# A long convolution with a top-2 FFN on one core: the last chunk cut into channel halves, under a new instruction order

## The chip, the cores and the metric

One core of a Trainium2 chip. The time is device microseconds of one execution, given as the median of several runs; a profile adds the trace of one execution, whose span is some 2 us shorter than the time. Executions of one kernel spread by several per cent (144.09 to 150.12 us for the changed kernel in one call), so I quote stage lengths from traces beside medians. The record calls an execution slow when it is over 1.5% above the fastest of its kernel in the same call; medians here are over all executions of a call, unless I say fast. Engines: PE multiplies matrices, DVE and ACT work on vectors, POOL is a third and slower one (an addition of 128x512 elements takes 1156 ns there and 426 on DVE, in the first profile), SP sends DMAs.

## The reference, cut to what matters

```python
h  = x + q_ln * (irfft(rfft(kv) * rfft(filter)) + kv * D)      # q_ln = layernorm(x), kv = short_conv(k) * v
r  = layernorm(h) @ w_r;  idx = top-2 tokens by r              # 2048 tokens, 640 channels
y  = (silu(sel @ w_gate) * (sel @ w_up)) @ w_down              # for the two selected tokens only
out = h + layernorm(h);   out[idx] += y * sigmoid(r[idx])
```

The rows to be selected are known only after every channel of `h` is done: the end of the convolution is on the path to everything that follows.

## The kernel before

The 640 channels go in five chunks of 128. A chunk has two forward transform stages (`S1`, `S2`), two elementwise products with the filter's spectrum (`P1`, `P2`), two inverse stages (`I1`, `I2`), a multiplication by q with an addition to x (`I2m`, `I2a`), a transposition of the new h (`T`), and Gram sums of the transposed h (`G`), which give the second layernorm's statistics and the scores. Matmul results are copied out of PSUM by ACT or DVE. Four PSUM regions are shared out by the plan.

The program is recorded as steps, and a list, `PLAN`, gives their order, the engine and the PSUM region of each; semaphores follow from the order. Each engine runs its steps in that order.

```python
# products of chunk c: two blocks of 64 frequencies, all channels
def p1(b):
    blk = slice(64 * b, 64 * b + 64)
    op("dve", lambda e: e.tensor_tensor(dst[:, :, blk], A[:, :, blk], dst[:, :, blk], ALU.mult), ...)
def p2(b): ...                         # the same for K (the swapped spectrum)
for b in range(2): p1(b)
for b in range(2): p2(b)
...
# first inverse, block gb of 32 channels: needs all frequencies, so both P1 and both P2
for gl in range(8):
    matmul(R32(bt)[...], lhsT=dst[:, g, :], rhs=G[:, 0, :], start=True, stop=False)
    matmul(R32(bt)[...], lhsT=K[:, g, :],   rhs=G[:, 1, :], start=False, stop=True)
# second inverse, tokens n0..n1, all 128 channels: needs all four copies of the first
for n2 in range(n0, n1):
    for cp in range(2):
        matmul(R32(bt)[...], lhsT=H[:, n2, cp, :], rhs=Bp[:, 16 * cp + n2, :], start=(cp == 0), stop=(cp == 1))
# (cut: copies, I2m, I2a, transposes, Gram sums, scheduler)
```

## Time and profile before

| | before |
|---|---|
| time, median of the first comparison | 152.75 us (152.32 to 154.05) |
| span of the first profile | 148.27 us |
| PE / DVE / ACT busy | 86 / 78 / 76 % |
| last forward stage begins | 99.18 us |
| last forward copy ends (point A) | 106.84 us |
| first inverse of the last chunk begins | 114.35 us, A + 7.51 |
| second inverse of the last chunk begins | 121.55 us, A + 14.71 |
| last Gram matmul ends | 131.78 us, A + 24.94 |
| from there to the end | 16.49 us |

I split the span at these points: "front" is the time to the start of the last forward stage, "segment" runs from there to the last Gram matmul, and "end" is the rest. The segment is 32.60 us here. The 40-slice part of the page shows PE's busy tenths, its granted clock and DMA:

```profile
PE   7397999958959599979999999999998979967962
...
PEclk9999999999999999999999999999999996985799
DMA  4999399937999979968865956853189934035980
```

Each digit is a slice of 3.7 us in tenths. PE is busy nearly everywhere, so a gain can come only from work that it does sooner, or at a better clock. The clock falls below full in the 34th slice (6), which lies inside the segment, and in the 36th to 38th (8, 5, 7), mostly behind it. The segment's own lines stand in the prediction.

### The profile page before, as it was taken

What the parts mean: (1) busy time and instruction counts of PE and PEld (TensorE: products, weight loads), DVE (VectorE), ACT (ScalarE), POOL (GpSimd) and SP (SyncE); (2) the same over time, 40 slices, a digit from 0 to 9 for tenths busy, and PEclk for the clock granted to TensorE, in tenths of its full rate; (3) what the DMA queues carried; (4) which work ended last, traced back from release to release, by engine and by line L of the source; (5) the groups of instructions that cost most, each with busy time, mean ns of one, the idle gap of its engine ahead of it and who ended that gap; (6) DMA issues with size and microseconds to landing.
All of it is one profiled execution on the core that took longest, in us unless ns stands there. A gap on an engine that the chain in (4) does not pass through costs nothing.

```text
span 148.3 us, 6818 instructions
## 1 busy us (share of the span) xinstructions
PE 127.6 (86%) x3087; PEld 113.3 (76%) x3087; DVE 115.0 (78%) x178; ACT 112.2 (76%) x133; POOL 31.8 (21%) x46
## 2 busy tenths in 40 slices
PE   7397999958959599979999999999998979967962
PEld 7256896657849499969989899898997879935950
DVE  0486779885898689699989998999899556478921
ACT  0596799399988958979898996889999902639910
POOL 2011004300170219067421506230600000000010
PEclk9999999999999999999999999999999996985799
DMA  4999399937999979968865956853189934035980
GB/s 108 335 287 372 78 334 393 226 81 219 257 162 240 240 205 222 230 179 304 178 137 121 213 111 147 180 206 123 47 265 337 317 111 124 4 93 171 427 322 6
DMA packets 20769, 30.07 MB, mean 203 GB/s; under 512 B 5311, under 2 KB 15748, under 8 KB 20228
## 3 DMA queue, kind: packets, MB, share of 16 engines
q1 hardware_dynamic: 20200, 28.03, 67.0%
q0 software_dynamic: 512, 1.60, 4.2%
q8 instruction: 24, 0.39, 1.2%
q14 instruction: 5, 0.04, 0.1%
q10 hardware_dynamic: 28, 0.00, 0.0%
HBM read 19.60 MB, written 2.62 MB: 150 GB/s over the span
## 4 chain that ended last, share of the span: by engine, by line
PE 49%; DMA 19%; DVE 13%; ACT 11%; issue 4%; SPq 1%; DVEq 0%
PE ps L622 9%; DMA big<-in_A_ssm_k_dram 7%; PE ps L666 6%; ACT A L350 6%; PE ps L597 5%; DMA big<-big 5%; DMA KfB<-A 4%; PE ps L729 4%; DMA q_sb<-c_F 4%; PE ps L711 3%; PE ps L712 3%; PE ps L1047 3%; DVE KfB L643 2%; PE ps L845 2%; DVE big L350 2%
## 5 line engine op out<-in xcount | busy, mean ns | idle before, releaser
L350 ACT ACTIVATE big<-ps 128x1024 bf16<-128x1024 f32 (+1 forms) x33 | 33.5, 1066 | 5.9 <-PE ps L622 5.7
L350 ACT ACTIVATE A<-ps 128x1024 bf16<-128x1024 f32 x33 | 31.5, 1036 | 3.1 <-PE ps L666 3.0
L666 PE MATMUL ps<-big,F 128*128 128x64 bf16 x640 | 22.0, 192 | 4.4 <-DVE big L350 2.2
L622 PE MATMUL ps<-F,big 128*64 128x128 bf16 x640 | 23.5, 228 | 2.5 <-DVE big L350 1.6
L666 PEld LDWEIGHTS ps<-big,F 128*128 128x128 bf16 x640 | 20.2, 97 | 5.7 <-ACT A L350 2.6
L622 PEld LDWEIGHTS ps<-F,big 128*64 128x64 bf16 x640 | 19.8, 115 | 5.3 <-DVE big L350 2.4
L711 PE MATMUL ps<-G,A 128*128 128x128 bf16 x160 | 19.2, 219 | 0.1
L712 PE MATMUL ps<-G,KfB 128*128 128x128 bf16 x160 | 19.2, 219 | 0.0
L802 POOL TENSOR_SCALAR q_sb<-x_sb,ln 128x640 bf16<-128x640 bf16 x16 | 14.1, 879 | 23.1 <-DVE A L687 11.6
L350 ACT ACTIVATE Bp<-ps 128x1024 bf16<-128x1024 f32 x16 | 15.6, 1055 | 1.1 <-PE ps L712 1.1
L711 PEld LDWEIGHTS ps<-G,A 128*128 128x128 bf16 x160 | 15.5, 98 | 0.8 <-DVE atmp L739 0.2
L350 ACT ACTIVATE q_sb<-ps 128x2048 bf16<-128x2048 bf16 (+2 forms) x7 | 9.7, 1427 | 8.3 <-PE ps L750 8.3
L712 PEld LDWEIGHTS ps<-G,KfB 128*128 128x128 bf16 x160 | 15.7, 98 | 0.0
L739 DVE TENSOR_TENSOR atmp<-q_sb,ps 128x1024 bf16<-128x1024 bf16 (+1 forms) x11 | 12.1, 1117 | 4.0 <-PE ps L729 3.8
L350 DVE COPY big<-ps 128x2048 bf16<-128x2048 bf16 (+1 forms) x10 | 11.2, 1118 | 4.5 <-PE ps L546 1.5
L607 DVE TENSOR_TENSOR big<-ps,big 128x1024 bf16<-128x1024 f32 x10 | 12.0, 1219 | 2.5 <-PE ps L597 2.4
L743 POOL TENSOR_TENSOR x_sb<-x_sb,atmp 128x512 bf16<-128x512 bf16 x8 | 9.1, 1156 | 17.2 <-DVE atmp L739 6.3
L695 DVE TENSOR_TENSOR KfB<-A,KfB 128x2048 bf16<-128x2048 bf16 x10 | 12.3, 1248 | 0.0
L687 DVE TENSOR_TENSOR A<-A 128x2048 bf16<-128x2048 bf16 x10 | 12.1, 1217 | 0.1
L729 PE MATMUL ps<-Bp,H 128*128 128x128 bf16 x160 | 11.3, 229 | 0.5 <-ACT Bp L350 0.4
L729 PEld LDWEIGHTS ps<-Bp,H 128*128 128x128 bf16 x160 | 9.9, 103 | 1.1 <-ACT Bp L350 0.5
L350 DVE CAST big<-ps 128x1024 bf16<-128x1024 f32 x8 | 9.5, 1217 | 1.5 <-PE ps L622 1.5
(131 smaller groups left out, 194.6 us busy)
## 6 DMA issues: line engine op xcount, KB each, us to landing
KfB<-A SPq DMA_DIRECT2D x6, 512.0 KB, 4.8
big<-big SPq DMA_DIRECT2D x10, 260.0 KB, 6.3
big<-in_A_ssm_k_dram SPq DMA_DIRECT2D x5, 512.0 KB, 5.1
out_dram<-q_sb SPq DMA_DIRECT2D x4, 640.0 KB, 4.7
big<-in_B_w_up_dram SPq DMA_DIRECT2D x5, 432.0 KB, 4.9
big<-in_B_w_gate_dram SPq DMA_DIRECT2D x5, 432.0 KB, 4.5
big<-in_A_k_dram SPq DMA_DIRECT2D x4, 512.0 KB, 4.2
big<-in_A_v_dram SPq DMA_DIRECT2D x4, 512.0 KB, 5.8
```

What stands on the lines that cost most here:

```text
L350: return flex(lambda e: e.activation(o, i(), ACTF.Copy), lambda e: e.tensor_copy(o, i()), reads, writes, (t_act(n), t_d2(n) if bf else t_d ...
L607: op("dve", lambda e: e.tensor_tensor(kv[:, :, 8 * hb:8 * hb + 8, :], R32(bt).rearrange("p (n g l) -> p g n l", n=8, l=4), v_T[:, 8 * hb:8 ...
L622: return e.matmul(R32(bt)[64 * cc:64 * cc + 64, 128 * gl:128 * gl + 128], lhsT=lt, rhs=F1[:, cc, :], start=True, stop=True, tile_position= ...
L666: bt = op("pe", [lambda e, kl=kl: e.matmul(R32(bt)[:, 64 * kl:64 * kl + 64].rearrange("p (s g) -> p s g", s=2), lhsT=F2[:, 16 * r + kl, :] ...
L687: op("dve", lambda e: e.tensor_tensor(dst[:, :, blk], A[:, :, blk], dst[:, :, blk], ALU.mult), reads=[buf("A2", ksl(c), r) for r in rs], w ...
L695: return lambda e: e.tensor_tensor(K[:, g0:g1, blk], A[:, g0:g1, blk], K[:, g0:g1, blk], ALU.mult)
L711: ems.append(lambda e, g=g, gl=gl: e.matmul(R32(bt)[:, 128 * gl:128 * gl + 128], lhsT=dst[:, g, :], rhs=G[:, 0, :], start=True, stop=False))
L712: ems.append(lambda e, g=g, gl=gl: e.matmul(R32(bt)[:, 128 * gl:128 * gl + 128], lhsT=K[:, g, :], rhs=G[:, 1, :], start=False, stop=True))
L729: ems.append(lambda e, n2=n2, nl=nl, cp=cp: e.matmul(R32(bt)[:, 128 * nl:128 * nl + 128], lhsT=H[:, n2, cp, :], rhs=Bp[:, 16 * cp + n2, :] ...
L739: tr.decl({"dve": lambda e: e.tensor_tensor(at, qv, R32(bt)[:, 0:128 * nn].rearrange("p (n d) -> p n d", n=nn), ALU.mult)}, qb, ab, {"dve" ...
L743: em["pool"] = [lambda e, a=a: e.tensor_tensor(xs[:, a:a + 4, :], xs[:, a:a + 4, :], at[:, a:a + 4, :], ALU.add) for a in range(0, nn, 4)]
L802: lambda e, n2=n2: e.tensor_scalar(q_sb[:, n2, :], x_sb[:, n2, :], rd[:, n2:n2 + 1], nb[:, n2:n2 + 1], op0=ALU.mult, op1=ALU.add),
```

## The change

The intent: let the last chunk's second half of channels be multiplied while the first half is already in the inverse stages, and let the residual end in small pieces.

```diff
+LASTG = True
+            def ph(h):                                  # products by halves of the channels, all frequencies
+                g = slice(NG // 2 * h, NG // 2 * h + NG // 2)
+                op("dve", lambda e: e.tensor_tensor(dst[:, g], A[:, g], dst[:, g], ALU.mult), ..., writes=[buf("P1o", h)], ...)
+                op("dve", lambda e: e.tensor_tensor(K[:, g], A[:, g], K[:, g], ALU.mult), ..., writes=[buf("P2o", h)], ...)
+            if last(c):
+                ph(0)
+                ph(1)
+                return
...
-            bt = op("pe", ems, reads=dbufs[0] + dbufs[1] + [buf("P2", c % 2, 0), buf("P2", c % 2, 1), bG], ..., name="I1%d%d" % (c, gb))
+            bt = op("pe", ems, reads=([buf("P1o", gb // 2), buf("P2o", gb // 2)] if last(c) else ...) + [bG], ..., name="I1%d%d" % (c, gb))
...
+        def b_I2h(c, h, n0, n1):                        # second inverse, 64 channels, tokens n0..n1
+            bt = op("pe", [lambda e, n2=n2, cp=cp: e.matmul(R32(bt)[...], lhsT=H[:, n2, cp, :], rhs=Bp[:, 16 * cp + n2, w * h:w * h + w], ...)
+                           for n2 in range(n0, n1) for cp in range(2)], reads=[buf("Bp", 2 * h), buf("Bp", 2 * h + 1), bH], ...)
+            ...                                         # I2m and I2a on the same half
...
-            for p_ in parts(c):
-                b_I2(c, *p_)
+            if last(c):
+                b_I2h(c, 0, 0, NB)                      # first half: all 16 token blocks
+                for p_ in parts(c):                     # second half: 8, 4, 4 token blocks
+                    b_I2h(c, 1, *p_)
+            else: ...
# cut: PLAN, replaced as a whole (559 steps before, 562 now)
```

The new list also moves things outside the last chunk. The first Gram chunk stands ahead of the last chunk's first inverse and the second between its blocks, instead of both behind it; the second chunk's filter is loaded ahead of eight token blocks of x; and the output normalizations stand elsewhere.

## The prediction

> **What bounds the kernel now.** I read the busy times first: TensorE (PE) 86% of the 148.3 us span, ScalarE (ACT) 76%, VectorE (DVE) 78%. Such averages name no bound: the 40 slices show all three at 0.9 in the middle and DVE and ACT falling to 0.2 to 0.6 after slice 30. The chain that ended last agrees:
>
> ```profile
> PE 49%; DMA 19%; DVE 13%; ACT 11%; issue 4%; SPq 1%; DVEq 0%
> ```
>
> So what a change to the last of five channel chunks is worth must be read between the last forward stage and the end of the Gram sums (the row sums and squares for the second layernorm, L845 and L850). The time-ordered list of DVE's instructions there:
>
> ```profile
> 107.15 2.48 DVE L643 COPY KfB<-A 64x4096 bf16<-64x4096 bf16 x2
> 109.66 1.23 DVE L687 TENSOR_TENSOR A<-A 128x2048 bf16<-128x2048 bf16 x1
> 110.80 2.35 DVE L695 TENSOR_TENSOR KfB<-A,KfB 128x2048 bf16<-128x2048 bf16 x2
> 113.07 1.22 DVE L687 TENSOR_TENSOR A<-A 128x2048 bf16<-128x2048 bf16 x1
> 114.21 2.34 DVE L739 TENSOR_TENSOR atmp<-q_sb,ps 128x1024 bf16<-128x1024 bf16 x2
> 118.37 1.23 DVE L350 CAST Bp<-ps 128x1024 bf16<-128x1024 f32 x1 [1.82 <-PE ps L712]
> 119.51 1.28 DVE L741 TENSOR_TENSOR x_sb<-x_sb,atmp 128x1024 bf16<-128x1024 bf16 x2
> 123.22 1.22 DVE L739 TENSOR_TENSOR atmp<-q_sb,ps 128x1024 bf16<-128x1024 bf16 x1 [2.43 <-PE ps L729]
> ```
>
> It is serial: swap 2.5 us, four products 4.6 us (each covers half the frequencies and all channels, so no inverse matmul may start before the fourth ends at 114.29), then DVE idles while PE does all 64 first-inverse matmuls, and idles again until the second inverse. The chain shows what PE did from 118.3:
>
> ```profile
> 118.33 0.31 PE ps L845 x32
> 118.64 0.28 PE ps L850 x8
> 118.92 0.25 PE ps L845 x22
> 119.17 0.83 issue
> ...
> 121.62 1.56 PE ps L729 x16
> 123.19 1.71 PE ps L750 x16
> 124.89 0.69 PE ps L729 x8
> ```
>
> The last Bp copy ends at 119.60, but the in-order PE queue holds two whole Gram chunks in front of the second inverse, which starts two microseconds late and then runs slowly. The windows tell why:
>
> ```profile
> 120.00:122.00 2.00, 2.00 (x105) 1.86 (x105) 0.79 (x2) 0.00 (x0) 0.00 (x0) 0.97 0.10 38
> 122.00:124.00 2.00, 2.00 (x22) 2.00 (x20) 0.78 (x1) 0.00 (x0) 0.00 (x0) 0.50 0.55 154
> 124.00:126.00 2.00, 2.00 (x57) 1.95 (x55) 1.51 (x3) 1.07 (x1) 0.00 (x0) 0.68 0.20 76
> ```
>
> The third figure from the right is the granted PE clock: half. The Gram sums end at 131.83; 16.5 us of dependent small steps (top-2 search, gather, FFN, row write) follow.
>
> [...] 0.50 follows a stretch of 32- and 2-column matmuls with a 0.83 us hole, and sixteen L729 matmuls take 1.56 us there, 0.89 to 1.00 elsewhere. [...] here sixteen 64-column matmuls (L666) take 0.47 us, 29 ns each, sixteen of 128 take 0.89 us, so splitting into 64 columns costs little. [...] the products take 1217 and 1248 ns on runs of 64, so halves by channel should cost the same. [...] The 0.83 us "issue" fell while DMA was 84% busy (118.2 to 120)[...].
>
> **The change, part by part.** Let A be the end of the last copy of the last forward stage (106.8 before). I lay the new order of each engine's queue out from A with durations of this trace.
>
> Products: still 4 x 1.2 us, but the first two finish channels 0 to 63. Ready at A + swap 2.5 + sign 0.1 + 2.4 = A+5.0; before, everything at A+7.5. The new order puts one residual multiply (1.2) between the pairs, so the second half is ready at A+9.2.
>
> First inverse: PE does chunk 3's four blocks, a transpose, Gram chunk 0 and chunk 3's second inverse until A+6.5; blocks 1 and 0 of the last chunk until A+8.3; Gram chunk 1 to A+9.4; blocks 2 and 3 to A+11.25 (PSUM regions come free just in time). Both Gram chunks thus move into PE's wait for products: in the old order they cost 118.33 to 121.55.
>
> Second inverse: first half 32 x 0.03 = 1.0, A+11.3 to A+12.3 (old: starts A+14.7). DVE multiplies it to A+13.5. PE meanwhile transposes chunk 3 and does eight tokens of the second half, then four, Gram 2, four (last ends A+15.3). DVE: 0.7 + 0.68 + 0.4 + 2 x 0.4 + 2 x 0.28 = 3.1 after A+13.65: residuals complete A+16.8 (my estimates for the smallest sizes, scaled from 0.42 at 512 elements). Last transposes, Gram 3 and 4: A+18.8. Added work: 32 more matmuls (1.94 against 1.78 us) and three short DVE instructions; trivial.
>
> Before, the same stretch took 131.83 - 106.8 = 25.0. Laid out with the same ideal durations it would be about 21.3: the other 3.7 are the half clock, the hole and small hand-overs. So the structure is worth 21.3 - 18.8 = 2.5 us; up to 3.7 more depends on whether the new queue avoids the cold clock. PE is nearly gapless from A to A+17 and the Gram sums are interleaved with dense matmuls, so I count half of it: 1.8. Together -4.3 us.
>
> Front: the plan is new everywhere. Summed with this trace's durations, ACT has 96.3 us of work up to its last forward copy in both orders, DVE 94.3 and 94.7 up to the swap: neither is relieved. Immediately before A, ACT gets all eight forward copies (8 x 1.03) where DVE took one, and DVE gets two transposed copies: A about 1 us later there. But the load of chunk 1's filter moves up by eight token blocks, 1.28 MB, an estimated 3.4 us at some 380 GB/s; this ended a wait of 2.5 us on ACT (29.68), and lies on the chain as "DMA big<-in_A_ssm_k_dram". I count -1 us net, the least certain term.
>
> Tail after Gram: the first four warm-up matmuls move from before the key transposes to the very end. They held up nothing (done 133.97, transposes at 134.13), and the clock was 0.50 there in spite of them. One output normalization (0.4) now stands before the row maximum and three instead of two between it and the second maximum (0.4 beyond the 0.7 of the transposes): +0.8 on the path to the gather. ACT does eight normalizations instead of seven before its table load and the sigmoid, +0.8, but the FFN's end was set by 1.12 us of "issue" at 141.86, so part hides there. Net +0.3. Weight loads are issued earlier except one up-projection and some down-projection loads; they are needed some 9 us later and land in about 5.
>
> Sum: -4.3 - 1.0 + 0.3 = -5.0 us on the span; 152.81 - 5.0 = 147.8. Hand-laid queues lose some at every hand-over, so I say 148.2.
>
> **Rivals.** (1) The clock goes cold anyway, and an instruction hole comes too: the end of the new order is still small Gram matmuls and transposes. [...] Then only structure is left, -2.5 - 1.0 + 0.3 = -3.2: about 149.6, within a hair of 2%. (2) DVE becomes the bound of the tail: 5.0 us of products and swap, the inserted multiply and nine short operations are one queue. Against: it still waits for PE at A+12.3 and twice was idle before (1.82, 2.43). If true, second-half residuals arrive 1 to 2 us later: 149.5. (3) The new front loses: loads in another order, stacked-shift DMAs, forward copies on ACT. At +2 us instead of -1: 151, called the same. (4) Everything works, clock warm and filter wait gone: 145.
>
> **Range and chances.** The front gives about +-2 us, clock and holes +-1.8, tail +-0.8; together about +-3: 145.0 to 151.4. The 2% line is 149.75; rivals 1 and 2 land just on its fast side, only a losing front or two of them together cross it. Faster 0.70, same 0.27, slower 0.03.
>
> **What would show it.** Right: two products end, then L711/L712 start some 2.5 us after the swap while the other two run; both early Gram chunks lie before the last first-inverse block; from A to the last Gram matmul 19 to 21 us instead of 25.0; clock at 1.0 until then; ACT's 2.5 us wait for the filter gone, A at or before 106.8; from Gram's end to the span's end 16 to 17.5. Wrong: A later than 108, the half clock already in the second inverse, or the last DVE residuals waiting in DVE's own queue.

## The result, and the profile after

The changed kernel takes 147.24 us (147.09 to 149.54) against 152.75 us. The ratio is 0.962, with a 95% interval of 0.956 to 0.968. Ratios are the mean time of one kernel's fast runs over that of the other's in the same rounds, so not quite the ratio of the medians. Its first profile fell on a slow execution (span 147.65 us); I read a second one (span 144.86 us) and a third (148.32, slow again). The spread is in the front and, in the third, at the end; the segment hardly moves. (A variant below with the same order up to the last Gram matmul, the output normalizations off the path, took 29.32 us for it.)

| us | before, 2 traces | changed, 3 traces |
|---|---|---|
| front | 99.18, 102.81 | 102.30, 99.30, 101.57 |
| segment | 32.60, 33.10 | 28.57, 28.75, 28.83 |
| end | 16.49, 16.44 | 16.78, 16.81, 17.92 |
| A to the first inverse | 7.51, 7.51 | 6.44, 6.34, 6.70 |
| A to the second inverse | 14.71, 14.67 | 11.19, 11.09, 11.45 |
| A to the last Gram matmul | 24.94, 25.43 | 19.97, 20.14, 20.22 |

DVE's instructions in order of time, changed kernel, second profile (start, length, engine, line, operation, tiles, shapes; in brackets idle time before and what ended it):

```profile
108.25 2.48 DVE L644 COPY KfB<-A 64x4096 bf16<-64x4096 bf16 x2
...
110.83 1.21 DVE L707 TENSOR_TENSOR A<-A 128x2048 bf16<-128x2048 bf16 x1
111.96 1.22 DVE L708 TENSOR_TENSOR KfB<-A,KfB 128x2048 bf16<-128x2048 bf16 x1
113.56 1.22 DVE L752 TENSOR_TENSOR atmp<-q_sb,ps 128x1024 bf16<-128x1024 bf16 x1 [0.37 <-PE ps L742]
114.69 1.22 DVE L707 TENSOR_TENSOR A<-A 128x2048 bf16<-128x2048 bf16 x1
115.83 1.22 DVE L708 TENSOR_TENSOR KfB<-A,KfB 128x2048 bf16<-128x2048 bf16 x1
...
120.14 2.05 DVE L770 TENSOR_TENSOR atmp<-q_sb,ps 128x1024 bf16<-128x1024 bf16 x2 [0.63 <-PE ps L764]
122.10 1.02 DVE L772 TENSOR_TENSOR x_sb<-x_sb,atmp 128x1024 bf16<-128x1024 bf16 x2
123.04 0.74 DVE L770 TENSOR_TENSOR atmp<-q_sb,ps 128x256 bf16<-128x256 bf16 x2
123.70 0.48 DVE L772 TENSOR_TENSOR x_sb<-x_sb,atmp 128x256 bf16<-128x256 bf16 x2
```

The four products still cost 1.2 us each, but the second one ends at 113.18 (A + 5.27), and PE, busy with the chunk before until then, starts the first inverse at 114.25 while the third and fourth products are still to come. The chain of waits of the same trace shows the second inverse and the last transposes and Gram matmuls (start, length, engine, line, count):

```profile
119.17 0.93 PE ps L764 x32
120.10 0.89 PE ps L777 x16
120.99 0.83 PE ps L764 x24
121.82 0.18 PE ps L877 x8
...
125.43 0.18 PE ps L877 x8
125.60 0.23 PE ps L872 x20
125.83 1.19 issue
127.02 0.25 PE ps L872 x12
...
127.46 0.26 PE ps L872 x16
```

L764 is the second inverse by halves, L777 the transposition, L872 and L877 the Gram sums. Thirty-two 64-column matmuls take 0.93 us; transposing sixteen blocks takes 0.89 us, where the kernel before needed 1.71 at a clock of 0.50. The windows have the clock third from the right, 1.00 here:

```profile
120.00:122.00 2.00, 2.00 (x62) 1.91 (x61) 1.73 (x2) 1.22 (x2) 0.00 (x0) 1.00 0.06 17
122.00:124.00 2.00, 2.00 (x111) 1.83 (x113) 2.00 (x7) 1.07 (x2) 0.00 (x0) 1.00 0.00 0
...
126.00:128.00 2.00, 0.98 (x52) 0.82 (x51) 0.26 (x1) 0.00 (x0) 0.00 (x0) 1.00 0.79 229
128.00:130.00 2.00, 0.05 (x9) 0.00 (x0) 1.90 (x9) 0.34 (x3) 0.20 (x1) 0.80 1.05 359
```

The clock stays full until after the last Gram matmul (it halves at 129.2; in the other two traces at 131.7 and 132.0, again 0.8 to 1.6 us after that matmul). In the two traces of the kernel before it halves at 121.9 and 124.9, inside the segment, for 3.4 us. What is left is one hole of 1.19 us called "issue" among the last Gram matmuls (0.91 and 0.92 in the other traces).

### The profile page after: what moved, and what is told of

It reads as the page before. It is cut to its first block, busy times and chain, and to the rows that moved or that the text cites.

```text
span 147.7 us, 6882 instructions
## 1 busy us (share of the span) xinstructions
PE 123.0 (83%) x3119; PEld 110.0 (75%) x3119; DVE 114.5 (78%) x185; ACT 109.7 (74%) x129; POOL 30.5 (21%) x45
## 4 chain that ended last, share of the span: by engine, by line
PE 53%; DMA 17%; ACT 11%; DVE 11%; issue 5%; SPq 1%; DVEq 0%
DMA KfB<-A 8%; ACT A L351 8%; PE ps L623 8%; PE ps L667 6%; PE ps L724 5%; PE ps L725 5%; DMA big<-big 5%; DMA q_sb<-c_F 4%; PE ps L742 4%; ACT big L351 3%; PE ps L777 3%; PE ps L524 3%; DVE big L351 3%; PE ps L1079 3%; PE ps L604 3%
## 5 line engine op out<-in xcount | busy, mean ns | idle before, releaser
L351 ACT ACTIVATE big<-ps 128x1024 bf16<-128x1024 f32 (+2 forms) x39 | 39.3, 1068 | 9.1 <-PE ps L623 8.8
L351 ACT ACTIVATE A<-ps 128x1024 bf16<-128x1024 f32 x31 | 29.4, 1047 | 2.4 <-PE ps L667 2.2
L725 PE MATMUL ps<-G,KfB 128*128 128x128 bf16 x160 | 18.8, 219 | 0.0
L756 POOL TENSOR_TENSOR x_sb<-x_sb,atmp 128x512 bf16<-128x512 bf16 x6 | 6.8, 1151 | 24.8 <-DVE KfB L699 13.1
L752 DVE TENSOR_TENSOR atmp<-q_sb,ps 128x1024 bf16<-128x1024 bf16 x8 | 9.7, 1218 | 2.2 <-PE ps L742 2.1
L691 DVE TENSOR_TENSOR A<-A 128x2048 bf16<-128x2048 bf16 x8 | 9.7, 1217 | 2.1 <-DMA KfB<-A 2.1
L351 DVE CAST A<-ps 128x1024 bf16<-128x1024 f32 x9 | 10.8, 1221 | 0.4 <-PE ps L667 0.3
L598 PE MATMUL ps<-diag,big 128*128 128x64 bf16 x256 | 8.6, 194 | 1.9 <-DMA big<-big 1.9
L524 PE MATMUL ps<-q_sb,cons 128*128 128x512 bf16 x20 | 6.8, 478 | 3.6 <-DMA q_sb<-c_F 3.6
L699 DVE TENSOR_TENSOR KfB<-A,KfB 128x2048 bf16<-128x2048 bf16 x8 | 9.8, 1231 | 0.0
L598 PEld LDWEIGHTS ps<-diag,big 128*128 128x128 bf16 x256 | 7.9, 98 | 2.4 <-issue 2.0
```

The costliest lines, as they stand in the source:

```text
L351: return flex(lambda e: e.activation(o, i(), ACTF.Copy), lambda e: e.tensor_copy(o, i()), reads, writes, (t_act(n), t_d2(n) if bf else t_d ...
L524: wt = op("pe", [lambda e, i=i: e.matmul(R32(wt)[:, 512 * (i % 2):512 * (i % 2) + 512], lhsT=ident, rhs=F2c[:, 0:16].rearrange("p k c m -> ...
L598: return e.matmul(R32(bt)[:, o:o + 64], lhsT=lt, rhs=diagS[:, s, h, a, :], start=(a == 0), stop=(a == 1))
L699: return lambda e: e.tensor_tensor(K[:, g0:g1, blk], A[:, g0:g1, blk], K[:, g0:g1, blk], ALU.mult)
L725: ems.append(lambda e, g=g, gl=gl: e.matmul(R32(bt)[:, 128 * gl:128 * gl + 128], lhsT=K[:, g, :], rhs=G[:, 1, :], start=False, stop=True))
L752: tr.decl({"dve": lambda e: e.tensor_tensor(at, qv, R32(bt)[:, 0:128 * nn].rearrange("p (n d) -> p n d", n=nn), ALU.mult)}, qb, ab, {"dve" ...
```

## The experiments

Line numbers of the variants are a few lower, since their lists are printed more tightly. All outputs are right. A variant with new tasks in the old places is made by giving a new `PLAN`; I show which steps move. The kernel before was timed beside each call, and its median there went from 150.70 to 153.25 us, so small differences between calls mean nothing.

**Both kernels again.**

> The changed kernel once more, for a profile in the fast state. Theory (the gain lies in the tail, from the last forward stage to the end of the Gram sums): ratio 0.955 to 0.968 as before, from the start of the last forward stage to the end of the last Gram matmul about 28 us against 32.6 in the old profile. Rival (the gain is in the front and the first profile of the changed kernel merely hid it): in a fast-state profile the last forward stage starts well before 99 us.

Measured: 147.82 us against 153.25, a ratio of medians of 0.965; the stages are in the table above. Only one of seven of the kernel before was fast, and at 147.84 us it lay among the three fast ones of the changed kernel (146.75 to 148.09). Over all calls the medians are 152.07 us (45 executions of the kernel before) and 147.56 us (15 of the changed one). The segment was as the theory said. The last forward stage started at 99.30, not well before 99: the gain isn't hidden in the front.

> The kernel before against itself: ratio 1.00 within 0.5 per cent. Its first profile was 2.4 us quicker than its median, so I expect a new profile with a span near 150.7 us; theory: the extra 2 us sit in the front as longer waits for DMA or for instructions, and the tail segment from last forward stage to last Gram matmul stays 31 to 33 us. Rival: the tail itself varies by 2 us.

Measured: 151.05 us median, and a slow profile of 152.35 us. The front took 3.6 us more than in the first profile (102.81 against 99.18) and the segment 33.10 against 32.60. So in these two traces the spread of one and the same kernel is in the front. Two traces of one kernel thus differ there by as much as I wanted to measure, and no single pair of traces can price the front. The same file against itself came out 2.2 us under the other runs of the kernel before in that call, not within the 0.5 per cent that I expected, which shows how far a median of five can be trusted here.

**Old front, new tail.** The seam is the end of the fourth chunk's forward stage, where both lists have done nearly the same steps.

```diff
-PLAN = new[0:334] + new[334:562]
+PLAN = old[0:334] + (the steps of new that are not in it, in new's order)
```

> Old order up to the end of the fourth chunk's forward stage (334 of 562 steps of the plan), then the new order with the halves. Theory of the prediction (tail -4, front -1): 148 to 149.5, ratio about 0.972. Rival all-tail: ratio 0.962. Rival all-front: ratio 0.99 to 1.00.

Measured: 147.98 us (147.89 to 151.23), median of 153.25 beside it; ratio of the medians 0.966. Segment 29.21 us (the clock halves at 128.4, 0.7 us before its end), front 99.91, end 16.78. The new tail behind the old front is as good as the whole change within what the spread allows (147.82 us in the same call). The ratio lies between the theory and the all-tail rival and doesn't part them.

**New front, old tail.**

```diff
-PLAN = old[0:334] + old[334:559]
+PLAN = new[0:334] + (the steps of old that are not in it, in old's order)
```

> New order up to the same seam, then the old order with undivided products, inverse stages and additions. Theory of the prediction: front alone is worth 1 us, 151 to 152, ratio about 0.99. Rival all-tail: 1.00. Rival all-front: 0.962 to 0.97.

Measured: 150.16 us (147.77 to 151.53), front 98.06, segment 31.49, end 16.42. The time, a ratio of medians of 0.980, lies between the theory and the all-front rival and settles neither. The segment is the instructive number. The same tail steps took 32.60 and 33.10 us behind the old front; here they took 31.49, and the clock was full:

```profile
120.00:122.00 2.00, 1.61 (x30) 1.49 (x28) 1.44 (x2) 0.04 (x1) 0.00 (x0) 1.00 0.68 187
122.00:124.00 2.00, 2.00 (x98) 1.89 (x96) 1.52 (x3) 1.84 (x1) 0.00 (x0) 1.00 0.12 43
124.00:126.00 2.00, 1.62 (x70) 1.45 (x69) 1.11 (x2) 1.51 (x2) 0.00 (x0) 1.00 0.00 0
```

The old tail can thus run without the half clock. Together with a third such trace (31.20 us, below) this parts the gain: 32.60 to 33.10 with the half clock, 31.20 to 31.49 without, so 1.1 to 1.9 us of clock; and 31.20 to 31.49 less 28.57 to 28.83, so 2.4 to 2.9 us of structure. These two traces also lack the 0.8 us hole in the early Gram sums; holes of 0.36 to 0.39 us stand elsewhere.

I could have read the parts from PE alone. The whole segment of the kernel before, of this one and of the changed one (after the length: PE busy, PE weight loads, DVE, ACT, POOL, clock, DMA):

```profile
99.18:131.78 32.60, 29.92 (x835) 28.04 (x832) 24.63 (x28) 23.38 (x23) 2.27 (x2) 0.95 0.50 159
98.06:129.55 31.49, 28.48 (x836) 26.46 (x832) 24.58 (x28) 23.38 (x23) 2.27 (x2) 1.00 0.50 162
99.30:128.05 28.75, 27.56 (x873) 26.60 (x869) 24.66 (x31) 20.88 (x21) 4.54 (x4) 1.00 0.59 178
```

The segment holds the same PE work in all three, but that in the changed kernel 64 matmuls of 64 columns stand for 32 of 128, and five of one column have moved in. At full clock PE's busy time falls by 1.4 us. Of its idle time, 2.7 to 3.2 us in the two traces of the kernel before, 1.5 us are waits for data; in the changed kernel none over 0.15 us is left, and the 0.9 to 1.2 us of idle are the holes. The other 0.8 us of busy time I can't part; ends of matmuls are modelled. So the changed segment is PE's own work plus one hole.

**Only the filter's early load, in the kernel before.**

```diff
 SP: ... vT01 vT00
+    fC1
     x5 x8 x0
-    fC1
     G ...
```

> The kernel before with one thing moved: the load of chunk 1's filter goes out right after chunk 0's v, ahead of eight token blocks of x. Theory: ACT's wait of 2.5 us for it before the first forward copy falls under 0.5 us, PE's hole of 1.65 us near 30 us is gone, the second forward stage starts 1 to 2 us sooner than 44.5 to 45.4, no half-clock window near 33 us, total ratio 0.985 to 0.995. Rival: the next wait (shifted copies by DMA) ends last anyway, the second chunk's forward stage starts no earlier, ratio 1.00.

Measured: 151.91 us against 151.25; the span of its profile was 151.63. The signs near 30 us came true: the filter's step on ACT starts at 26.99 instead of 29.68, the wait of 2.52 us and PE's hole of 1.65 us are gone, and there is no half clock at 33 us (the second trace of the kernel before has it). Still nothing came of it: the second chunk's last forward stage starts at 44.89, against 44.48 and 45.38. The chains of waits, first of the kernel before, then of this one:

```profile
19.95 9.71 DMA big<-in_A_ssm_k_dram
29.66 0.02 issue
29.68 0.30 ACT big L543
...
45.04 6.93 DMA big<-big
```

```profile
19.48 10.10 DMA x_sb<-in_A_q_dram
29.61 4.83 DVE st L800 x12
...
45.44 6.95 DMA big<-big
```

The eight token blocks now land last, DVE's statistics of x start at 29.61 instead of 26.84, and the shifted-copy DMA starts at 45.44 instead of 45.04. The rival's outcome came, for another reason than it gave: DMA is full here (a share of 0.96 or more from 18 to 30 us in both traces), so the load sent sooner made another land later. (Its segment, 31.20 us with the clock full, is the third trace used above; the execution was slow.)

**The new order without the halves.** Products by frequencies, inverse stages and additions undivided, each put where the new list has the piece that it replaces.

```diff
 DVE: ... P140 P240 I2m30 P141 P241 ...          # same places; each now covers all channels, half the frequencies
-PE:  I240(half 0, 16 blocks) T3 I240(half 1, 8) I2412 G2 I248 T4 ...
+PE:  I240(8 blocks)          T3 I248            I2412 G2      T4 ...
```

> The new order everywhere, but products by frequency halves over all channels, undivided inverse stages and additions as before. Theory (halves are what allow the overlap, order alone is not enough): the first inverse can't start before the fourth product, some 3 us later after the last forward copy than in the changed kernel (6.4), PE idles about 2 us, from the start of the last forward stage to the last Gram matmul about 31 us against 28.7, time about 149.8. Rival (order alone does it, the halves are ornament): 28.5 to 29.2 us, time 147.5.

Measured: 150.80 us against 151.25 (ratio 1.004, interval 0.967 to 1.040). Segment 33.31 us, first inverse at A + 9.22: 2.5 to 2.9 us later than in the changed kernel, as the theory had it. The segment was even longer than the 31 us that I had written down, and the windows show both the wait and what follows it:

```profile
114.00:116.00 2.00, 1.33 (x24) 1.15 (x21) 1.60 (x3) 0.29 (x1) 0.00 (x0) 1.00 0.34 80
116.00:118.00 2.00, 0.00 (x0) 0.00 (x0) 2.00 (x3) 0.00 (x0) 0.00 (x0) 1.00 0.45 169
118.00:120.00 2.00, 1.98 (x26) 1.99 (x27) 1.97 (x3) 0.81 (x1) 0.00 (x0) 0.72 0.00 0
120.00:122.00 2.00, 2.00 (x90) 1.90 (x88) 0.42 (x1) 1.24 (x2) 0.00 (x0) 0.50 0.03 8
```

PE stands still for 2.7 us, since the inserted residual multiplication (1.2 us) now lies ahead of products that every block needs, and the clock halves at 118.9. The new order as it stands, without the halves, is no better than the old kernel. This doesn't rule out every order without halves: the old one with only the Gram sums moved was not run. Its trace shows little room for that, since between A and the first inverse PE is idle for only 0.36 us.

**The halves without the new Gram places.**

```diff
-PE: ... T2 G0 I230 I238 I141 I140 G1 I142 I143       I240 ...
+PE: ... T2    I230 I238 I141 I140    I142 I143 G0 G1 I240 ...
```

> The changed kernel with the first two Gram chunks put back between the first and the second inverse, as in the kernel before. Theory: PE waits about 2 us among the first-inverse blocks, then spends 2.3 us on Gram sums before the second inverse: same segment 30.5 to 31.5 us against 28.7; the half clock may return inside it. Rival (the halves alone do it): 28.5 to 29.2 us.

Measured: 149.91 us against 151.25 (ratio 1.009, interval 0.988 to 1.031). Segment 32.56 us. Its chain of waits:

```profile
117.44 0.30 PE ps L868 x32
...
119.72 0.95 PE ps L760 x29
120.67 0.72 issue
121.39 0.25 PE ps L760 x3
...
124.68 0.81 issue
...
128.74 0.84 issue
```

The first inverse starts early (A + 5.64), PE waits 1.15 us for the second pair of products, and the Gram sums then hold the second inverse up to A + 12.90 instead of 11.1 to 11.5: a good part of the 4 us. Besides, three holes of 0.72, 0.81 and 0.84 us follow and the clock halves at 126.8. My expectation was 1 to 2 us too low; I had no holes in it, and these come to 2.37 us against 0.9 to 1.2 in the changed kernel. So in one trace each, neither half of the change shortens the segment alone (33.31 and 32.56 against 32.60 to 33.10), and together they are worth 4 us. The halves alone did bring the second inverse 1.8 us forward (A + 12.90 against 14.7) and lost it again to holes and clock; whether another execution would lose it too is not tested.

**The output normalizations off the path.**

```diff
-DVE: ... keyi outn max1 outn outn outn max2 oh      sprod      outn acc      outn ...
+DVE: ... keyi      max1 outn outn      max2 oh outn sprod outn      acc outn outn ...
```

> The changed kernel with the output normalizations moved off the path: none before the row maximum, two between it and the second maximum. Theory: from the last Gram matmul to the start of the gather 5.0 us become about 4.0 (3.76 in the old kernel), the rest after it keeps its length; total 0.8 to 1.0 us under the changed kernel, 146.5. Rival: the later instruction fetches or the weights' arrival end the FFN and take the gain back: same as the changed kernel.

Measured: 149.10 us (146.31 to 150.93) against 151.25, not the 146.5 that I expected. From the last Gram matmul to the gather 4.60 us, where the changed kernel takes 5.01 and the kernel before 3.79. That is 0.4 us, half of what I expected. The result row was complete 13.45 us after the last Gram matmul (13.63 and 13.88 in the changed kernel's first two traces), but the row's DMA then ended 3.42 us later instead of 2.9 to 3.2, and the end was 16.87 us, no shorter. The trace shows why, and it is not the rival that I wrote down: the row was complete at 143.12, the last output store landed at 143.80, and the row's write was issued at 144.10. The row may be written only after the output stores, and the last of them landed 14.13 us after the last Gram matmul, against 14.04 and 14.06 in the changed kernel.

**The weights' last loads, earlier and later.** The remaining hole of about 1 us lay where three loads of the down-projection run.

> The changed kernel beside the two variants on one chip: ratio to the kernel before 0.955 to 0.985 (the spread seen so far), from the start of the last forward stage to the last Gram matmul 28.5 to 29.3 us, a hole of 0.9 to 1.2 us called issue among the last Gram matmuls.

Measured: 148.90 us (144.09 to 150.12) against 152.63; ratio 0.967, interval 0.945 to 0.988, which counts as unclear beside the 2% line; segment 28.83, hole 0.92. In this trace the second FFN matmul ran at half clock and took 2.05 us instead of 1.22, after a hole of 1.08 us, and the end was 17.92 us.

```diff
-SP: ... wg                      | T4: wd | T4: wd wd | last G4: wu wd | stores
+SP: ... wg wd wd wd wu wd (all behind G1) |                            | stores
```

> The changed kernel with its last five weight loads (1.8 MB) sent right after the second Gram chunk, some 5 to 9 us sooner, into a stretch where DMA is under 10 per cent busy. Theory (the hole among the last Gram matmuls is PE waiting for a block of instructions whose fetch shares the DMA engines with these loads): the hole is gone or under 0.4 us, the segment is 27.5 to 28.2 us, the kernel 0.7 to 1.2 us faster than the changed one. Rival (the hole is the fetch itself, whatever else DMA does): the hole stays at 0.9 to 1.2 us, same time as the changed kernel.

Measured: 150.23 us against 152.63 (ratio 1.002, interval 0.990 to 1.014), 1.3 us above the median of the changed kernel beside it; of each, two executions were fast, 147.81 and 149.39 against 144.09 and 145.91. Segment 30.23 us. Chain and windows of this kernel:

```profile
122.51 0.25 PE ps L760 x5
122.76 1.68 issue
124.44 0.34 PE ps L760 x3
```

```profile
122.00:124.00 2.00, 0.76 (x45) 0.58 (x42) 1.06 (x3) 0.52 (x1) 0.00 (x0) 1.00 1.04 369
124.00:126.00 2.00, 1.56 (x51) 1.55 (x51) 0.82 (x3) 0.33 (x1) 0.00 (x0) 0.62 0.37 132
```

The hole did leave the Gram sums, and stood 3 us earlier, in the second inverse (L760), under the loads that I had moved, and longer: 1.68 us while DMA was full. The trace has the packets of the instruction queue: in the changed kernel's second profile such blocks start at 116.5, 120.6 and 124.1, each taking 1.1 to 1.3 us; here at 116.2 and only then at 122.1. PE stands still from 122.76 to 124.44, behind the block that began at 122.1, and the clock halves at 124.5.

> Both the early weights and the output normalizations off the path to the gather. Theory: 27.5 to 28.2 us for the segment, then 0.4 us less to the gather, of which the first try of that kept 0.2 to 0.3 by the end of the row; 1.0 to 1.5 us faster than the changed kernel. Rival: the final row write waits for the output stores, which start no sooner, and nothing of the 0.4 us remains.

Measured: 150.18 us against 152.63; segment 32.13 with a hole of 2.75 us in the same place, gather 4.55 us after the last Gram matmul. The loads' harm covers whatever the normalizations gave.

```diff
-SP: ... wg | T4: wd | T4: wd wd | last G4: wu wd          | stores
+SP: ... wg |                    | last G4: wu wd wd wd wd | stores
```

> The opposite move: the three down-projection loads that the changed kernel sends among the last transposes and Gram matmuls go out after the last Gram matmul. Theory (the hole called issue follows these loads): no hole over 0.4 us between the last second-inverse matmul and the last Gram matmul, segment from the start of the last forward stage 27.4 to 28.0 us against 28.6 to 28.8, after it no more than 17.3 us; time 0.3 to 1.0 us under the changed kernel's 147.2 to 148.9. Rival (instruction fetch is late there in any case): hole 0.9 to 1.2 us as before, segment 28.6 or more. A third outcome: hole gone but output stores or the FFN late by as much.

Measured: 150.71 us (149.34 to 151.39) against 150.70. The segment is 28.76 us, that of the changed kernel, and the hole is there although DMA is idle:

```profile
128.00:130.00 2.00, 1.09 (x70) 0.89 (x72) 0.53 (x3) 0.00 (x0) 0.00 (x0) 1.00 0.00 0
```

```profile
128.01 0.23 PE ps L868 x20
128.24 0.91 issue
129.15 0.25 PE ps L868 x12
```

So about 0.9 us of the hole is not the loads' doing; in the two kernels whose loads run over a fetch it was 1.68 and 2.75 us. That the holes are waits for instruction blocks, all traces support: 34 holes of over 0.3 us called issue lie behind 100 us in the fourteen traces, and in each PE goes on 1.0 to 1.6 us after the packets of its queue's last block ended, 2.2 to 3.0 us after they began. Why a block comes 0.9 us late with DMA idle is argued only: the changed kernel's second profile has 224 matmuls and weight loads in the 2 us from 122, so by my estimate a block of some 257 instructions (the 6174 matmuls and weight loads of the kernel before over the 24 instruction packets of PE's queue on its page) lasts 2.3 us there, against 6.6 us in the first inverse (78 in the 2 us from 114). No run changed that rate alone. The end grew to 18.59 us, since the loads now run into the output stores and the row's DMA ended 4.47 us after the row.

## Why the prediction was right

**The total.** 148.2 us was predicted, 147.24 measured in the first comparison, 147.82 and 148.90 in the later ones. The parts summed to 147.8; the other 0.4 us was my allowance. Part of the closeness is luck: the stretch from A gave more than forecast, and the front, by what the traces can tell, less.

**Products and first inverse.** "Ready at A+5.0", second half "at A+9.2", first blocks from A+6.5: the second product ended at A + 5.27 and the fourth at A + 9.14 in the second profile, and the first inverse began at A + 6.34 to 6.70. The products took 1216 to 1248 ns each in the mean, whichever way they were cut (first profiles of both kernels). Right.

**Second inverse.** Predicted A+11.3, measured 11.09 to 11.45; 32 matmuls in 0.93 us for a predicted 1.0. Right. That the Gram sums had to move for this is shown by the run with them in the old place (12.90), and that this order needs the halves by the undivided run (16.41). One reading was off: "PE's wait for products", into which the Gram sums move, is no wait of the old order, where PE was busy with the chunk before; it comes with the halves (1.15 us in the run with the Gram sums in the old place).

**End of the segment.** Ideal A+18.8, with an unknown share of 3.7 us of clock and holes. Measured 19.97 to 20.22. The clock part was avoided altogether in these traces, the hole was not: 0.91 to 1.19 us of the excess is the one hole. In the kernel before the clock halved 2.7 and 2.1 us after holes of 0.83 and 0.77 us began amid 32- and 2-column matmuls; two traces of the same tail without those holes (31.49 and 31.20 us) kept the full clock there, as did the changed kernel, whose holes of 0.91 to 1.19 us come at the very end of its Gram sums. What share the hole has in it and what the small matmuls, no run here shows; to count half of the 3.7 us for a queue with few gaps was my estimate. From A, where the -4.3 us starts, the stretch shrank from 24.94 and 25.43 to 19.97 to 20.22, by 5.1 us between the means: the mechanism was right, the size 0.8 us too small. Beside the two old tails at full clock (A + 23.54 and 23.83), 3.3 to 3.9 us of it is structure, for which I had put 2.5, and 1.1 to 1.9 clock and the hole before it (1.8). The segment shrank by less, 4.1 us between the means, because the last forward stage up to A took 8.60 us instead of 7.66; the prediction had that under the front ("A about 1 us later there").

**Front.** -1.0 us was called the least certain term, and its reasoning failed: the early filter takes the wait away but not the time, because x lands later (the prediction's 380 GB/s is an estimate; the first trace of the kernel before shows 324 to 406 from 18 to 26 us). The start of the last forward stage is 99.9 us in the mean of ten traces with the new front (98.06 to 102.30) and 101.2 in four with the old (99.18 to 102.81), a difference of 1.3 us that the spread doesn't settle. The first comparison's 5.5 us exceed what segment and end account for in the traces (4.1 - 0.3 = 3.8 us, from the first two traces' ends), so some 1.7 us lie in the front or in chance. Counted up to A, as the prediction's -1.0 is, that is 0.8 us. Its stages changed: the second chunk's forward stage to the third's takes 17.57 and 17.05 us in the first two traces of the changed kernel, 18.88 and 21.09 before. Which of its many moves did that is not tested.

**End.** +0.3 us was predicted, and 0.3 came in two traces, but by luck: the path was wrong. The way to the gather grew by 1.2 us (5.01 against 3.79), not 0.8. I had overlooked that in the kernel before the sums of the first twelve token blocks were reduced while PE still waited for the last transposition; in the changed kernel the three last Gram parts end together, so all reductions lie on the path. But neither this path nor the FFN set the end. In both traces of the kernel before and the first two of the changed one the row's write is issued 0.29 to 0.31 us after the last output store landed, and 0.5 to 1.3 us after the row was complete. That store landed 13.80 and 13.85 us after the last Gram matmul before and 14.04 and 14.06 in the changed kernel, and the write then took 2.35 and 2.44 us: that is the 0.3. In the third trace the row came last, with a hole and the half clock in the FFN, and the end was 1.1 us longer.

**Rivals.** The half clock (1) did not come (1.00 up to the last Gram matmul), the hole did (0.91 to 1.19 us). DVE as the bound (2) is not borne out: it is idle 0.63 us before the second inverse's multiplication and 1.05 us before the last copies. The losing front (3) is visible in single executions, as it is with the kernel before.

## What to carry to other kernels

Cutting a stage in halves and reordering the queue each gained nothing measurable here, in one trace each, and 4 us together: the halves make early work possible, and the queue must have room for it and fill the wait with what used to stand in front of it. Lay both orders out from a common point with measured durations, and compare the ideal old order, not the measured one, with the ideal new one; the rest is clock and fetch (here 1.1 to 1.9 and 0.9 to 1.2 us), to be priced apart. On a full DMA (a share of 0.96 or more) the load sent sooner made another land later, and DVE started on x at 29.61 us instead of 26.84: ask which. Keep bulk loads away from long runs of small matmuls: a hole among them was 0.91 us with DMA idle, 1.68 and 2.75 with loads filling it. And ask of the end of a kernel what lands last; a shorter path to the row was worth nothing while the output stores came after it.
